# An attention and mixture-of-depths kernel: x stored in halves, weight blocks and mixing at new places, five broadcast loads of 1/rms begun on GpSimd's queue

## The chip, the cores and the metric

The kernel runs on one core of one Trainium2 chip. The core has five engines that each work through their own list of instructions in order: TensorE (PE, matrix products and transposes; PEld in the profile is its weight load), VectorE (DVE), ScalarE (ACT), GpSimd (POOL) and SyncE (SP, here only an issuer of DMA transfers). Engines wait for each other by semaphores. Sixteen DMA engines carry the transfers. The metric is the device time of one execution in microseconds (us); lower is better.

## The reference

The inputs are q, k, v of shape (B 8, H 12, S 448, D 64), the gains g_q and g_k, a gate vector and two matrices of a small network. What is computed:

```
q, k   = rmsnorm(q) * g_q, rmsnorm(k) * g_k        # over D
p      = exp(q k^T / sqrt(D));  x = (p v) / sum(p)  # full attention, no mask
x      -> (B, S, 768)                               # heads side by side
score  = x . w_gate                                 # one number per token
chosen = the 128 tokens of each batch with the highest score
y      = relu(x[chosen] w1) w2                      # 768 -> 1024 -> 768
out    = x, and at the chosen tokens x + sigmoid(score) * y
```

All of it is float32.

## The kernel before

**Groups.** The 96 heads are worked in 24 groups n of four heads; three groups make a batch. A group has seven chunks of 64 keys per head, called units here: `scores` (L404, TensorE) gives the product of keys and queries of one chunk, ScalarE takes its exponential (L413), `values` (L428, TensorE) multiplies by v and accumulates. The main loop runs over q = 0 to 23, one group per round, with `values` trailing `scores` by two or three chunks. PSUM gives `scores` four banks.

**Denominators.** VectorE adds up the probabilities of the chunks (`add_probs`, L444). The last ARRAY[n] chunks of group n are left out of that, and TensorE sums them in `sum_keys` (L471) beside VectorE's sum. `invert_sums` (L496) then forms the reciprocal, and `to_tokens` (L526 transposes on TensorE, L528 products on VectorE) lays the result out by tokens in `xs[b]`, two pieces c = 0 and 1 for each group.

**1/rms.** The norm of the queries of group n is not applied before the scores are due, but as late as possible, in a chain over four engines and a detour by memory: `squares` (L298, ScalarE, sq0 for queries and sq1 for keys), `sum_squares` (L330 on VectorE, then the power of -0.5 at L331 on GpSimd), `rows_out` (L342, SyncE: 1/rms of the queries written to DRAM as rows), `rows_in` (L354: two loads hh = 0 and 1 of 224 KB each that spread the rows over 64 partitions, the tile `bc`), and `scale_q` (L363, VectorE: qT times bc). Only then can `scores` of group n start. Groups 0 and 1 are scaled in another way, without the detour. The norm of the keys goes into the exponential as its scale, so the power of sq1 must have ended before that.

**Queue order.** SyncE issues nearly all transfers, one after the other; an issue that must wait holds all that are behind it. The loads of qT and kT wait until the buffer's last reader, the scores of three groups earlier, has ended; v waits likewise for values of three groups earlier, tok (the rows for the squares, two loads per group) for squares of two groups earlier. `rows_in` waits until the rows have landed in DRAM.

**The planner.** Everything beside the loop's fixed order is put in `todo` under a slot: a number whose whole part is the round and whose fraction is the place in it. For q < 8 (FIRST) a round runs its entries at two points, A (0.5) and its end; later rounds at MID 0.4, P0 0.6, P1 0.75 and P2 0.9. Entries that fall between two run points are issued together, in the order of their slots. `prepare(n)` gives the steps of 1/rms default slots, and the table PREPARED overrides them; LOADS overrides the slots of loads, GATES and RANKS those of the gate sums and of the ranking, BLOCKS those of the 14 weight parts (256 to 512 KB each), MIXED those of `mix`.

**The small network.** After a batch's last tokens, `gate` (L554) and `spread` (L567) form the scores of all tokens, `score_rows` (L584) makes them rows, `count` (L600) ranks each token by how many are higher, `select` (L627, GpSimd) writes the chosen tokens to DRAM by four indirect transfers, and `load_selected` (L650) reads them back. `mixture` handles two batches at a time and does each layer with seven block products in place of eight (L753, L823), using sums and differences of weight blocks that `mix` (L292, VectorE) makes once and `store_mixed` and `load_mixed` take to DRAM and back. It is cut into pieces; rounds q >= 8 run one at each of P0, P1 and P2 unless SKIP names the place. The store of a finished x (L542, 1344 KB) is issued in `store_x` as soon as a batch's tokens are complete.

The lines that carry the slots of 1/rms are these:

```
times = {
    "sq0": n - 3 + (END if n - 3 < FIRST else P0),
    "out": n - 2 + (A if n - 2 < FIRST else P0),
    "in": n - 2 + (A if n - 2 < FIRST else P2),
    "scale": n - 1 + (A if n - 1 < FIRST else P0),
}
```

Of the kernel before, what the change touches and what calls it, by code (L numbers as in the profile page):

```python
# [17 lines left out]
def _bcast_row(ap_1d: bass.AP, parts: int) -> bass.AP:  # L18
# [1 line left out]

ARRAY = (0, 0, 1, 2, 3, 2, 2, 2, 1, 0, 0, 2, 1, 0, 0, 0, 0, 0, 0, 0, 0, 0, 0, 0)
GATE_PE = {1}
OTHER_BANK = (8, 12, 14, 15, 17, 20, 21)
SKIP = ((8, 0), (8, 1), (8, 2), (11, 2), (13, 2), (14, 1), (16, 2), (18, 2), (19, 2), (20, 1),
 (21, 1), (22, 1), (23, 1), (23, 2))
MIXED = ((1, 1, 0, 8.9), (1, 1, 1, 8.9), (1, 2, 0, 9.9), (1, 2, 1, 10.3), (1, 3, 0, 10.3),
 (1, 3, 1, 10.3), (1, 0, 0, 10.9), (1, 0, 1, 11.6), (2, 1, 0, 11.9), (2, 1, 1, 11.9),
 (2, 2, 0, 12.6), (2, 2, 1, 12.6), (2, 3, 0, 12.75), (2, 3, 1, 14.3), (2, 0, 0, 14.3),  # L30
 (2, 0, 1, 14.6))
BLOCKS = (2.3, 2.73, 3.16, 3.59, 4.02, 4.45, 4.88, 5.31, 4.74, 6.17, 6.6, 8.03, 7.46, 8.14)
LOADS = {('kT', 21): 19.3, ('tok', 15): 10.7, ('v', 18): 16.91}
PREPARED = {3: {'out': 1.3},
 4: {'in': 2.9, 'out': 2.3},
 5: {'in': 3.9, 'out': 3.3, 'sq1': 3.5, 'sum0': 2.92, 'sum1': 3.89},
 6: {'in': 4.9, 'out': 4.3, 'scale': 5.5},
 7: {'in': 5.9, 'out': 5.3},
 8: {'in': 6.9, 'sum1': 6.89},
 9: {'in': 7.9, 'out': 7.3},  # L40
 10: {'in': 8.9, 'out': 8.3},
 11: {'sum1': 9.75},
 13: {'scale': 12.59},
 14: {'scale': 13.4, 'sum0': 11.62},
 15: {'out': 13.75},
 17: {'in': 15.75},
 18: {'in': 16.92, 'out': 16.61},
 20: {'out': 18.89, 'scale': 19.42},
 22: {'out': 20.59},
 23: {'sq0': 20.76}}  # L50
GATES = {7: (8.9, 9.4),
 8: (9.9, 10.4),
 10: (11.75, 12.6),
 11: (12.9, 13.3),
 13: (15.3, 15.4),
 17: (18.75, 18.9),
 19: (20.9, 21.3),
 20: (21.9, 22.4),
 22: (24.4, 24.4)}
RANKS = {3: (13.6, 13.6, 13.6, 14.4), 5: (19.6, 20.4, 20.4, 20.9), 6: (22.9, 23.4, 23.4, 23.6)}  # L60


MAX_SCORE = 60.0
# [54 lines left out]
def fast(  # L118
# [21 lines left out]
    nc = tc.nc  # L140
# [3 lines left out]
    NJ = S // CP  # L144
# [4 lines left out]
    DM = H * D  # L149
# [7 lines left out]
    scale = 1.0 / math.sqrt(D)  # L157
# [190 lines left out]
    def rows_in(n):  # L348

        rows = bcs[n]  # L350
        bc = norm_pool.tile([128, 2, S], F32, name="bc")
        for hh in range(2):
            src = rows[hh].rearrange("(c s) -> c s", c=2)
            nc.sync.dma_start(  # L354
                out=bc[D * hh : D * (hh + 1)],
                in_=dataclasses.replace(src, ap=[[0, D]] + [list(x) for x in src.ap]),
            )
        bcs[n] = bc
# [35 lines left out]
    probs, sums, avs, xTs, rdens, xs = {}, {}, {}, {}, {}, {}  # L394
# [62 lines left out]
    def by_array(n):  # L457

        return ARRAY[n]

# [58 lines left out]
    def to_tokens(n, c, pool):  # L519
        b = n // NG  # L520
        if b not in xs:
            xs[b] = x_pool.tile([CP, NJ, DX], F32, name="x")
        t = xTs.pop((n, c))
        ps = bank(pool, [128, NJ, 128], "x_ps")
        for j in range(NJ):
            nc.tensor.transpose(out=ps[:CP, j, :], in_=t[:, j, :], identity=ident)  # L526
        col = (n % NG * 2 + c) * 128
        nc.vector.tensor_tensor(  # L528
            out=xs[b][:, :, col : col + 128].rearrange("p j (h d) -> p j h d", d=D),
            in0=ps[:CP].rearrange("p j (h d) -> p j h d", d=D),  # L530
            in1=rdens[n][:, :, :, c, None].to_broadcast([CP, NJ, 2, D]),
            op=OP.mult,
        )
        if c == 1:
            after_tokens(n)
# [2 lines left out]

    gates, parts, rowss, highers, ranks, slots_dram = {}, {}, {}, {}, {}, {}

    def store_x(b):
        nc.sync.dma_start(  # L542
            out=out[b].rearrange("(p j) c -> p j c", j=NJ), in_=xs[b][:, :, 0:DM]
        )

    def gate(n, js):
# [325 lines left out]
    def at(slot, fn, *args):  # L872
        todo.setdefault(slot, []).append(lambda: fn(*args))
# [3 lines left out]
    def soon():  # L877

        return slot[0] if now[0] < n_groups else -9
# [5 lines left out]
    def prepare(n):  # L885
        sq = {}
        times = {
            "sq0": n - 3 + (END if n - 3 < FIRST else P0),
            "sum0": n - 3 + END + 0.03 if n - 3 < FIRST else n - 2 + MID,
            "sq1": n - 2 + A if n - 2 < FIRST else n - 2 + P0 if n - 3 < FIRST else n - 3 + P1,  # L890
            "sum1": n - 2 + END + 0.02 if n - 2 < FIRST else n - 2 + MID,
# [16 lines left out]
        at(times["scale"], scale_q, n)

    for n in range(1, n_groups):  # L910
        if n > 2:
            for i in range(2):
                at(LOADS.get(("tok", n), n - 5 + P2 if n > 5 else (n - 3) * 0.6), load, "tok", n, i)
        if n > 1:
            at(LOADS.get(("qT", n), max(n - 3 + 0.1, 0.3)), load, "qT", n)
            at(LOADS.get(("kT", n), max(n - 2 + A, 0.3)), load, "kT", n)
            at(LOADS.get(("v", n), max(n - 2 + A, 0.3)), load, "v", n)
            prepare(n)
    for k, (l, b) in enumerate([(1, b) for b in kept + ((0, 1),)] + [(2, b) for b in kept]):
        for part in range(2):  # L920
            at(BLOCKS[2 * k + part], load_block, l, b, part)
    for l, i, part, t in MIXED:
        at(t, mix, l, i, part)
# [7 lines left out]
    def after_tokens(n):  # L931
        b, g = divmod(n, NG)
        s = soon()
        if g == NG - 1:
            at(s, store_x, b)
        if b in GATE_PE or g == 0:
            return
        q = now[0]
        if s < 0:
            t = [s, s]  # L940
        elif q < FIRST:
            t = [q + A, q + A] if g == NG - 1 else [q + END, q + END]
        else:
            t = [q + P2, q + 1 + MID]
        t = GATES.get(n, t)
        at(t[0], gate, n, (0, 1))
        at(t[1], gate, n, (2, 3))
        if g == NG - 1:
            at(t[1], spread, b)

    def ranks_of(b):
# [9 lines left out]
        else:  # L961
            times = [q + P2, q + 1 + MID, q + 1 + MID, q + 1 + P2]
            if b not in GATE_PE:
                times = [q + P0, q + P1, q + P1, q + 1 + 0.3]
        times = RANKS.get(b, times)
        at(times[0], count, b, (0, 1))
# [22 lines left out]
    def add_late():  # L989
# [7 lines left out]
        out=gg, in0=loads.gcol[:, 0:1], scalar=scale, in1=loads.gcol[:, 1:2], op0=OP.mult, op1=OP.mult  # L997
# [94 lines left out]
    n = n_groups - 1  # L1092
# [567 lines left out]
```

## Time and profile before

| | |
|---|---|
| median of 6 runs | 505.15 us (504.28 to 506.44) |
| the profiled execution's own time | 506.53 us, span 504.8 us |
| mean granted TensorE clock | 0.989 |
| busy, share of the span | PE 95%, PEld 59%, DVE 74%, ACT 57%, POOL 38% |
| DMA | 118.44 MB, 235 GB/s on average |
| bc: issue to landing | 3.3 / 4.5 / 12.4 us (min, median, max) |
| kT: issue to landing | 4.4 / 6.1 / 8.6 us |
| v: issue to landing | 5.1 / 7.0 / 9.1 us |

The rounds start (first `scores` of the group) at 10.4, 24.3, 36.9, 51.7, 65.7, 82.2, 98.3, 113.7, 127.5 and 143.4 us for q = 0 to 9, then about every 18 to 21 us, the last at 407.2. The profile is read with TensorE first: where it is never idle, only less work on it or a better order of the end can help; where it is idle, the bracket in its timeline names what it waited for, and the waits of the other engines lead back from there. A wait can be put down to the wrong engine when several semaphores end close together, so times of the instructions themselves decide.

### The profile page before, as it was taken

What the parts mean: (1) busy time and instruction counts of PE and PEld (TensorE: products, weight loads), DVE (VectorE), ACT (ScalarE), POOL (GpSimd) and SP (SyncE); (2) the same over time, 40 slices, a digit from 0 to 9 for tenths busy, and PEclk for the clock granted to TensorE, in tenths of its full rate; (3) what the DMA queues carried; (4) which work ended last, traced back from release to release, by engine and by line L of the source; (5) the groups of instructions that cost most, each with busy time, mean ns of one, the idle gap of its engine ahead of it and who ended that gap; (6) DMA issues with size and microseconds to landing.
All of it is one profiled execution on the core that took longest, in us unless ns stands there. A gap on an engine that the chain in (4) does not pass through costs nothing.

```text
span 504.8 us, 11762 instructions
## 1 busy us (share of the span) xinstructions
PE 479.3 (95%) x4716; PEld 295.4 (59%) x4716; DVE 371.8 (74%) x646; ACT 285.3 (57%) x523; POOL 191.7 (38%) x104
## 2 busy tenths in 40 slices
PE   7999998889979999999999999999999999999992
PEld 6553443445438785554556776655655577759951
DVE  5676887658987997888979886789988786743141
ACT  4877777577857647628557666656655663102100
POOL 0785440845753256404554237224445011021003
PEclk9999999999989999999999999999999999999996
DMA  8868989897998694878787698659385504864721
GB/s 292 314 193 284 268 256 311 271 271 244 309 312 255 227 320 160 275 261 280 243 269 262 217 355 260 207 194 309 131 273 203 173 7 137 271 225 162 229 87 67
DMA packets 44865, 118.44 MB, mean 235 GB/s; under 512 B 10147, under 2 KB 10404, under 8 KB 44802
## 3 DMA queue, kind: packets, MB, share of 16 engines
q1 hardware_dynamic: 41170, 110.66, 66.8%
q0 software_dynamic: 3344, 6.71, 3.7%
q8 instruction: 39, 0.64, 0.5%
q10 hardware_dynamic: 288, 0.23, 0.2%
q14 instruction: 24, 0.20, 0.1%
HBM read 93.81 MB, written 31.64 MB: 249 GB/s over the span
## 4 chain that ended last, share of the span: by engine, by line
PE 70%; DMA 4%; DVE 2%; issue 1%; POOL 1%; ACT 0%; SPq 0%; POOLq 0%; DVEq 0%
PE sc L404 17%; PE av L428 17%; PE moe_ps L753 9%; PE moe_ps L823 8%; PE side_ps L823 6%; PE side_ps L753 6%; PE x_ps L526 3%; PE den_ps L471 2%; DMA bc<-rows 2%; PE xeT_ps L729 1%; DMA rows<-rinv 1%; DMA out_dram<-xe,row 1%; PE row_ps L584 1%; POOL out_dram L683 1%; DVE prod L554 0%
## 5 line engine op out<-in xcount | busy, mean ns | idle before, releaser
L413 ACT ACTIVATE p<-sc,rinv 128x448 f32<-128x448 f32 x336 | 187.7, 641 | 88.1 <-PE sc L404 62.9
L331 POOL TENSOR_TENSOR rinv<-ss,neg_half 128x14 f32<-128x14 f32 x46 | 132.2, 2885 | 161.5 <-DVE ss L330 147.2
L404 PE MATMUL sc<-qT,kT 64*64 64x448 f32 x1344 | 155.4, 544 | 9.4 <-ACT sq L298 2.3
L428 PE MATMUL av<-p,v 64*64 64x448 f32 x1344 | 151.5, 539 | 0.0
L444 DVE TENSOR_TENSOR sum<-sum,p 128x896 f32<-128x896 f32 x104 | 113.7, 1094 | 5.3 <-ACT p L413 0.9
L404 PEld LDWEIGHTS sc<-qT,kT 64*64 64x64 f32 x1344 | 58.7, 133 | 72.9 <-issue 40.7
L428 PEld LDWEIGHTS av<-p,v 64*64 64x64 f32 x1344 | 64.3, 134 | 63.2 <-issue 54.6
L627 POOL DMA_INDIRECT selected<-x,rank x32 | 39.9, 1248 | 86.2 <-DVE x L619 78.7
L330 DVE TENSOR_REDUCE ss<-sq 128x14 f32<-128x910 f32 x46 | 48.8, 1093 | 3.6 <-ACT sq L298 3.6
L298 ACT ACTIVATE sq<-tok 128x896 f32<-128x896 f32 (+1 forms) x49 | 44.8, 936 | 8.8 <-DVE ss L330 4.8
L528 DVE TENSOR_TENSOR x<-x_ps,rden 112x512 f32<-112x512 f32 x48 | 32.6, 689 | 15.0 <-PE x_ps L526 12.9
L363 DVE SCALAR_TENSOR_TENSOR qT<-qT,gg,bc 128x896 f32<-128x896 f32 x22 | 25.5, 1161 | 18.2 <-DMA bc<-rows 18.2
L554 DVE SCALAR_TENSOR_TENSOR prod<-x,wg 112x448 f32<-112x448 f32 (+1 forms) x56 | 31.2, 557 | 1.4
L526 PE MATMUL x_ps<-ident,xT 128*112 128x128 f32 x192 | 28.5, 275 | 0.4 <-DVE rden L496 0.4
L444 DVE TENSOR_TENSOR sum<-p 128x896 f32<-128x896 f32 x24 | 26.1, 1087 | 3.5 <-ACT p L413 3.4
L683 POOL DMA_INDIRECT out_dram<-xe,row x7 | 8.4, 1200 | 52.0 <-DVE xe L695 45.8
L451 ACT COPY xT<-av 128x448 f32<-128x448 f32 x48 | 23.3, 538 | 3.7 <-PE av L428 3.2
L526 PEld LDWEIGHTS x_ps<-ident,xT 128*112 128x112 f32 x192 | 21.5, 133 | 4.8 <-issue 2.9
L753 PE MATMUL moe_ps<-xeT,ring 128*128 128x128 f32 x192 | 23.2, 277 | 0.2 <-DVE hT L770 0.2
L600 DVE SCALAR_TENSOR_TENSOR cmp<-score_rows,gate,earlier 112x448 f32<-112x448 f32 x32 | 21.8, 683 | 1.7 <-ACT score_rows L590 1.0
L753 PE MATMUL side_ps<-xeT,w 128*128 128x128 f32 x192 | 22.8, 275 | 0.0
L753 PEld LDWEIGHTS moe_ps<-xeT,ring 128*128 128x128 f32 x192 | 22.1, 192 | 1.0 <-issue 0.5
(106 smaller groups left out, 445.7 us busy)
## 6 DMA issues: line engine op xcount, KB each, us to landing
tok<-in_tok_dram SPq DMA_DIRECT2D x47, 448.0 KB, 6.1
ring<-mixed SPq DMA_DIRECT2D x48, 384.0 KB, 4.0
qT<-in_qT_dram SPq DMA_DIRECT2D x24, 448.0 KB, 4.0
kT<-in_kT_dram SPq DMA_DIRECT2D x24, 448.0 KB, 6.1
v<-in_vp_dram SPq DMA_DIRECT2D x24, 448.0 KB, 7.0
out_dram<-x SPq DMA_DIRECT2D x8, 1344.0 KB, 9.5
bc<-rows SPq DMA_DIRECT2D x44, 224.0 KB, 4.5
mixed<-ring SPq DMA_DIRECT2D x16, 384.0 KB, 5.8
```

The lines of the kernel that those rows point to most:

```text
L298: nc.scalar.activation(out=sq[:, h, :, 0:D], in_=t[:, h], func=AF.Square, scale=scale)
L330: nc.vector.tensor_reduce(out=ss, in_=sq, axis=AX.X, op=OP.add)
L331: nc.gpsimd.tensor_tensor(out=rinv.rearrange(flat), in0=ss.rearrange(flat), in1=neg_half.to_broadcast([128, 2 * NI]), op=OP.pow,)
L404: nc.tensor.matmul(out=scs[hh][D * c : D * (c + 1), 0:S], lhsT=get("kT", n)[r, c, D * i : D * (i + 1)], rhs=get("qT", n)[r, c, :], start=True,
L413: nc.scalar.activation(out=p[:, hh], in_=scs[hh][:, 0:S], func=AF.Exp, scale=rinvs[n, 1][:, hh, i : i + 1],)
L428: nc.tensor.matmul(out=avs[n][c][D * hh : D * (hh + 1), 0:S], lhsT=get("v", n)[r, hh, i, :], rhs=probs[u][r, hh], start=(i == 0), stop=(i ...
L444: nc.vector.tensor_tensor(out=sums[n], in0=probs.pop(u - 1) if begins else sums[n], in1=probs.pop(u), op=OP.add)
L526: nc.tensor.transpose(out=ps[:CP, j, :], in_=t[:, j, :], identity=ident)
L528: nc.vector.tensor_tensor(out=xs[b][:, :, col : col + 128].rearrange("p j (h d) -> p j h d", d=D), in0=ps[:CP].rearrange("p j (h d) -> p j ...
L627: w = nc.gpsimd.indirect_dma_start(out=t[:, :], out_offset=bass.IndirectOffsetOnAxis(ap=rank[:, j : j + 1], axis=0), in_=x[:, j, :], in_of ...
L753: nc.tensor.matmul(out=ps[:, 128 * f : 128 * f + n], lhsT=w[:, d, 128 * f : 128 * (f + 1)], rhs=h[:, d, :n], start=first and f == d == 0, ...
L823: nc.tensor.matmul(out=ps[:n, c0:c1], lhsT=h[:, f, :n], rhs=w[:, f, c0:c1], start=first and f == 0, stop=(f == HF - 1), skip_group_check=True,
```

## The change

Six tables and three small functions change. In words:

- Five of the 44 halves of `rows_in`, named in OTHER_QUEUE as (group, half), are begun on GpSimd's queue and no longer on SyncE's. GpSimd then waits for the rows to land before it goes on with what is behind.
- `store_x` issues a batch's store in two halves, and STORES gives four batches slots of their own for them; the other batches issue both halves where the whole one stood.
- BLOCKS and MIXED: 14 weight parts and 16 mixing steps get other slots, most of the parts later.
- LOADS: some 35 loads get slots of their own, above all qT 4, 6, 7, 9 to 11 and kT 10 to 14 and 16 to 18 later; PREPARED: the steps of 1/rms of most groups move, many `in` and `sq0` earlier.
- ARRAY: group 1 gives TensorE one chunk more, 5 two fewer, 6 one more, 11 one fewer, 12 one more; 16 in all in both. OTHER_BANK, GATES, RANKS and SKIP: other places for a PSUM bank, for gate sums, for ranking steps and for two of the pieces.

```diff
-ARRAY = (0, 0, 1, 2, 3, 2, 2, 2, 1, 0, 0, 2, 1, 0, 0, 0, 0, 0, 0, 0, 0, 0, 0, 0)
+ARRAY = (0, 1, 1, 2, 3, 0, 3, 2, 1, 0, 0, 1, 2, 0, 0, 0, 0, 0, 0, 0, 0, 0, 0, 0)
 GATE_PE = {1}
-OTHER_BANK = (8, 12, 14, 15, 17, 20, 21)
-SKIP = ((8, 0), (8, 1), (8, 2), (11, 2), (13, 2), (14, 1), (16, 2), (18, 2), (19, 2), (20, 1),
- (21, 1), (22, 1), (23, 1), (23, 2))
+OTHER_BANK = (8, 14, 20, 21)
+SKIP = ((8, 0), (8, 1), (8, 2), (11, 1), (13, 2), (14, 1), (16, 2), (18, 2), (20, 1), (22, 0),
+ (22, 1), (22, 2), (23, 1), (23, 2))
+OTHER_QUEUE = ((2, 0), (6, 0), (8, 1), (12, 0), (14, 0))
...
-BLOCKS = (2.3, 2.73, 3.16, 3.59, 4.02, 4.45, 4.88, 5.31, 4.74, 6.17, 6.6, 8.03, 7.46, 8.14)
-LOADS = {('kT', 21): 19.3, ('tok', 15): 10.7, ('v', 18): 16.91}
...
+BLOCKS = (3.55, 5.8, 3.16, 3.66, 4.27, 7.95, 7.13, 8.13, 6.24, 10.92, 6.1, 11.03, 9.71, 9.71)
+LOADS = {('kT', 5): 3.3,
+ ('kT', 10): 8.91,
+ ('kT', 11): 9.91,
+ ('kT', 12): 11.0,
+ ('kT', 13): 11.91,
+ ('kT', 14): 12.91,
+ ('kT', 16): 14.7,
+ ('kT', 17): 16.0,
+ ('kT', 18): 16.3,
+ ('qT', 3): 0.3,
+ ('qT', 4): 1.6,
+ ('qT', 6): 3.3,
+ ('qT', 7): 4.6,
+ ('qT', 8): 4.9,
+ ('qT', 9): 6.6,
+ ('qT', 10): 7.21,
...
+ ('v', 9): 8.0,
...
-PREPARED = {3: {'out': 1.3},
- 4: {'in': 2.9, 'out': 2.3},
- 5: {'in': 3.9, 'out': 3.3, 'sq1': 3.5, 'sum0': 2.92, 'sum1': 3.89},
- 6: {'in': 4.9, 'out': 4.3, 'scale': 5.5},
- 7: {'in': 5.9, 'out': 5.3},
- 8: {'in': 6.9, 'sum1': 6.89},
- 9: {'in': 7.9, 'out': 7.3},
- 10: {'in': 8.9, 'out': 8.3},
...
+PREPARED = {2: {'in': 0.51, 'sum1': 0.91},
+ 3: {'in': 1.5, 'out': 1.3, 'scale': 2.32, 'sq1': 1.3},
+ 4: {'in': 2.9, 'out': 2.3, 'sq0': 1.51},
+ 5: {'in': 3.51, 'out': 3.3, 'scale': 4.32, 'sq1': 3.5, 'sum1': 3.91},
+ 6: {'out': 4.3, 'scale': 5.5, 'sq0': 3.52, 'sq1': 4.29},
+ 7: {'in': 5.51, 'out': 5.3, 'sq0': 4.32},
+ 8: {'in': 6.51, 'out': 6.32, 'scale': 7.5, 'sum1': 6.89},
+ 9: {'sq0': 6.5, 'sq1': 7.5, 'sum1': 7.52},
+ 10: {'scale': 9.89, 'sq0': 7.49, 'sq1': 8.61, 'sum1': 8.61},
...
+ 15: {'out': 13.62, 'scale': 14.76, 'sq0': 12.89},
...
+STORES = {1: (6.9, 7.5), 2: (9.75, 10.75), 4: (15.75, 16.6), 6: (21.75, 22.6)}
...
-            nc.sync.dma_start(
+            queue = nc.gpsimd if (n, hh) in OTHER_QUEUE else nc.sync
+            queue.dma_start(
                 out=bc[D * hh : D * (hh + 1)],
...
-    def store_x(b):
+    def store_x(b, js):
         nc.sync.dma_start(
-            out=out[b].rearrange("(p j) c -> p j c", j=NJ), in_=xs[b][:, :, 0:DM]
+            out=out[b].rearrange("(p j) c -> p j c", j=NJ)[:, js], in_=xs[b][:, js, 0:DM]
         )
...
-            at(s, store_x, b)
+            for js, t in zip((slice(0, 2), slice(2, 4)), STORES.get(b, (s, s))):
+                at(t, store_x, b, js)
```

More of the change, by code (lines that the diff above doesn't have):

```diff
@@ L19, in _bcast_row @@
     return dataclasses.replace(ap_1d, ap=[[0, parts]] + [list(x) for x in ap_1d.ap])
-ARRAY = (0, 0, 1, 2, 3, 2, 2, 2, 1, 0, 0, 2, 1, 0, 0, 0, 0, 0, 0, 0, 0, 0, 0, 0)
+ARRAY = (0, 1, 1, 2, 3, 0, 3, 2, 1, 0, 0, 1, 2, 0, 0, 0, 0, 0, 0, 0, 0, 0, 0, 0)
 GATE_PE = {1}
-OTHER_BANK = (8, 12, 14, 15, 17, 20, 21)
-SKIP = ((8, 0), (8, 1), (8, 2), (11, 2), (13, 2), (14, 1), (16, 2), (18, 2), (19, 2), (20, 1),
- (21, 1), (22, 1), (23, 1), (23, 2))
-MIXED = ((1, 1, 0, 8.9), (1, 1, 1, 8.9), (1, 2, 0, 9.9), (1, 2, 1, 10.3), (1, 3, 0, 10.3),
- (1, 3, 1, 10.3), (1, 0, 0, 10.9), (1, 0, 1, 11.6), (2, 1, 0, 11.9), (2, 1, 1, 11.9),
- (2, 2, 0, 12.6), (2, 2, 1, 12.6), (2, 3, 0, 12.75), (2, 3, 1, 14.3), (2, 0, 0, 14.3),
- (2, 0, 1, 14.6))
@@ L32 @@
-BLOCKS = (2.3, 2.73, 3.16, 3.59, 4.02, 4.45, 4.88, 5.31, 4.74, 6.17, 6.6, 8.03, 7.46, 8.14)
-LOADS = {('kT', 21): 19.3, ('tok', 15): 10.7, ('v', 18): 16.91}
-PREPARED = {3: {'out': 1.3},
- 4: {'in': 2.9, 'out': 2.3},
- 5: {'in': 3.9, 'out': 3.3, 'sq1': 3.5, 'sum0': 2.92, 'sum1': 3.89},
- 6: {'in': 4.9, 'out': 4.3, 'scale': 5.5},
- 7: {'in': 5.9, 'out': 5.3},
- 8: {'in': 6.9, 'sum1': 6.89},
- 9: {'in': 7.9, 'out': 7.3},
- 10: {'in': 8.9, 'out': 8.3},
[L42 to L55, printed above, removed]
+OTHER_BANK = (8, 14, 20, 21)
+SKIP = ((8, 0), (8, 1), (8, 2), (11, 1), (13, 2), (14, 1), (16, 2), (18, 2), (20, 1), (22, 0),
+ (22, 1), (22, 2), (23, 1), (23, 2))
+OTHER_QUEUE = ((2, 0), (6, 0), (8, 1), (12, 0), (14, 0))
+MIXED = ((1, 1, 0, 8.9), (1, 1, 1, 9.9), (1, 2, 0, 9.3), (1, 2, 1, 10.3), (1, 3, 0, 10.3),
+ (1, 3, 1, 10.9), (1, 0, 0, 10.9), (1, 0, 1, 11.6), (2, 1, 0, 11.9), (2, 1, 1, 12.6),
+ (2, 2, 0, 12.6), (2, 2, 1, 12.6), (2, 3, 0, 13.6), (2, 3, 1, 14.6), (2, 0, 0, 14.4),
+ (2, 0, 1, 14.6))
@@ new lines @@
+BLOCKS = (3.55, 5.8, 3.16, 3.66, 4.27, 7.95, 7.13, 8.13, 6.24, 10.92, 6.1, 11.03, 9.71, 9.71)
[15 more added lines that the diff above has]
+ ('qT', 10): 7.21,
+ ('qT', 11): 8.6,
+ ('qT', 18): 15.6,
+ ('qT', 19): 16.6,
+ ('qT', 20): 17.21,
+ ('qT', 21): 18.3,
+ ('tok', 14): 9.5,
+ ('tok', 15): 10.7,
+ ('tok', 19): 15.4,
+ ('tok', 21): 17.4,
+ ('tok', 23): 18.5,
+ ('v', 3): 1.91,
+ ('v', 9): 8.0,
+ ('v', 10): 8.61,
+ ('v', 13): 11.91,
+ ('v', 15): 13.61,
+ ('v', 16): 14.3,
+ ('v', 18): 16.91,
+ ('v', 23): 21.1}
@@ new lines @@
+PREPARED = {2: {'in': 0.51, 'sum1': 0.91},
[7 more added lines that the diff above has]
+ 10: {'scale': 9.89, 'sq0': 7.49, 'sq1': 8.61, 'sum1': 8.61},
+ 11: {'sum0': 8.89},
+ 12: {'in': 10.92, 'scale': 11.74, 'sq0': 9.9},
+ 13: {'in': 11.74, 'scale': 12.6, 'sq0': 10.9, 'sum0': 11.4, 'sum1': 11.61},
+ 14: {'out': 12.62, 'scale': 13.6, 'sum0': 11.74},
+ 15: {'out': 13.62, 'scale': 14.76, 'sq0': 12.89},
+ 16: {'in': 14.74, 'out': 14.59, 'scale': 15.4, 'sq1': 14.4, 'sum1': 14.59},
+ 17: {'in': 15.61, 'sum0': 15.39},
+ 18: {'in': 16.92, 'scale': 17.61, 'sq0': 15.4, 'sq1': 16.4, 'sum0': 15.4},
+ 19: {'sq0': 16.91, 'sum1': 17.4},
+ 20: {'out': 18.76, 'scale': 19.42, 'sq0': 17.42},
+ 21: {'out': 19.75, 'scale': 20.74},
+ 22: {'out': 20.59, 'scale': 21.75},
+ 23: {'in': 21.74, 'out': 21.4, 'sum1': 22.6}}
@@ L56 @@
+STORES = {1: (6.9, 7.5), 2: (9.75, 10.75), 4: (15.75, 16.6), 6: (21.75, 22.6)}
+GATES = {8: (10.4, 10.4),
+ 10: (11.9, 12.75),
+ 11: (12.75, 12.75),
+ 14: (16.3, 16.4),
  17: (18.75, 18.9),
  19: (20.9, 21.3),
- 20: (21.9, 22.4),
- 22: (24.4, 24.4)}
-RANKS = {3: (13.6, 13.6, 13.6, 14.4), 5: (19.6, 20.4, 20.4, 20.9), 6: (22.9, 23.4, 23.4, 23.6)}
+ 20: (21.75, 22.3),
+ 22: (24.3, 24.9)}
+RANKS = {2: (10.9, 10.9, 10.9, 11.3), 5: (19.6, 20.3, 20.3, 20.4), 6: (22.9, 23.4, 23.4, 23.9)}
 MAX_SCORE = 60.0
```

## The prediction

> **What bounds the kernel now.** I read first the busy time by stretch, then the waits, then TensorE's own timeline where it sat idle, then SyncE's queue, and last the chain that ended last. Columns of the first view: stretch, its length, busy us of PE, PEld, DVE, ACT and POOL (instructions in brackets), granted clock, DMA share, GB/s.
>
> ```profile
> 0.00:150.00 150.00, 135.35 (x1618) 69.93 (x1622) 107.88 (x181) 105.95 (x190) 76.06 (x41) 0.99 0.86 277
> 150.00:430.00 280.00, 279.77 (x2738) 176.29 (x2731) 235.46 (x402) 171.05 (x318) 104.64 (x51) 1.00 0.69 229
> 430.00:505.00 75.00, 64.20 (x366) 49.19 (x365) 28.43 (x64) 8.29 (x16) 10.99 (x13) 0.95 0.50 170
> 143.00:150.00 7.00, 6.01 (x38) 2.12 (x42) 6.86 (x13) 3.24 (x6) 4.66 (x1) 0.76 1.02 370
> ```
>
> From 150 to 430 us TensorE is full, and a load that comes sooner is worth nothing there. The tail has 10.8 us of idle TensorE, but the change leaves the last products and writes as they are, and both versions run 34 pieces of the mixture in the loop. What can be won lies before 150 us, where 14.65 us are idle, 10.1 of them in the seven gaps shown below. The last row shows a granted clock of 0.76: in the trace it stands at 0.5 from 145.49 to 148.90 us.
>
> ```profile
> DVE qT L363 <- DMA bc<-rows: 18.2, 8, 4.2
> PEld den_ps L471 <- DVE sum L444: 11.0, 13, 1.7
> ```
>
> All eight of VectorE's waits for `bc` (the broadcast 1/rms) come before 150 us: 3.12 for group 2, then 2.67, 0.31, 2.25, 4.24, 3.86, 0.44 and 1.34 for groups 3 to 9. They reach TensorE directly (`scores` need the scaled qT) or through the sums and gates queued behind the scale:
>
> ```profile
> 44.90 0.59 PE L471 MATMUL den_ps<-sum,pick_pair 128*32 128x112 f32 x16 [0.83 <-DVE sum L444]
> 58.85 0.59 PE L471 MATMUL den_ps<-sum,pick_pair 128*32 128x112 f32 x16 [0.89 <-DVE sum L444]
> 81.67 0.56 PE L584 MATMUL row_ps<-ident,gate 112*112 112x112 f32 x4 [2.12 <-DVE gate L567]
> 98.33 0.98 PE L404 MATMUL sc<-qT,kT 64*64 64x448 f32 x8 [1.86 <-issue]
> 113.66 1.36 PE L404 MATMUL sc<-qT,kT 64*64 64x448 f32 x12 [1.47 <-ACT sq L298]
> 143.35 1.93 PE L404 MATMUL sc<-qT,kT 64*64 64x448 f32 x10 [2.26 <-DVE qT L363]
> 145.92 1.02 PE L404 MATMUL sc<-qT,kT 64*64 64x448 f32 x3 [0.64 <-DVE x L528]
> ```
>
> The gap is in the bracket. The labels at 98.33 and 113.66 mislead: the scale of group 6 ended at 98.23, that of group 7 at 113.56, each 0.1 us before. Why `bc` is late stands in SyncE's queue, which issues strictly in order:
>
> ```profile
> 64.39 0.33 SPq L110 DMA_DIRECT2D qT<-in_qT_dram  x1
> 65.30 0.36 SPq L342 DMA_DIRECT2D rows<-rinv  x1
> 70.74 1.09 SPq L354 DMA_DIRECT2D bc<-rows  x2
> 78.19 0.33 SPq L110 DMA_DIRECT2D qT<-in_qT_dram  x1
> 78.61 0.38 SPq L342 DMA_DIRECT2D rows<-rinv  x1
> 80.52 0.69 SPq L542 DMA_DIRECT2D out_dram<-x  x1
> 83.60 2.50 SPq L354 DMA_DIRECT2D bc<-rows  x2
> ```
>
> At 64.39 qT 6 had waited for the last scores of group 3 (64.32); rows 5, whose 1/rms was ready at 61.99, stood behind it. The same at 78.19: rows 6 were ready at 74.98. Then the 1344 KB store of x and two weight parts go out ahead of bc 6, which lands only at 96.96. So it is also on the chain (start, us, what):
>
> ```profile
> 126.56 3.80 DMA rows<-rinv
> 130.94 11.11 DMA bc<-rows
> 142.14 1.15 DVE qT L363
> ```
>
> **The change, part by part.** The profiled execution took 506.53 us (span 504.8); the median of the six runs is 505.15, 1.38 below. The sum is made against the former and taken off the latter.
>
> *Loads of qT behind rows.* qT 4, 6, 7 and 9 go behind `rows_out` of the group before them. Rows 3 leave about 1.4 us sooner (35.6 for 37.05) and their bc 3 lands near 47 instead of 50.37, before VectorE asks for it at 47.8: the 2.67 us wait goes, and with it the gaps at 51.72 (0.29) and 58.85 (0.89). What was queued behind qT (kT, v, weights) goes no later; qT itself is needed a whole group later, 0.33 us of issue each. Rows 5 leave at about 62.4 for 65.30, bc 5 at about 73 for 78.1; VectorE is ready at 75.9, so the 2.25 us wait goes and the row transposes' 2.12 with it. Next late there is VectorE itself: its gates end 2.2 us sooner.
>
> *bc 6 and bc 7.* Rows 6 leave near 75.7, and no store and fewer weights stand ahead. The rows give a landing of about 2 us plus the queued bytes at 290 GB/s (2.2 MB ahead of bc 7 took 9.4 us); that puts bc 6 near 85 against the 92.8 at which VectorE waits: 1.86 goes. For bc 7 the rows can't leave sooner (its 1/rms ends at 100.67, behind four row writes of the selection on GpSimd), but 512 KB of weights are gone from in front: about 108.5 for 112.4, with VectorE ready at 108.55: 1.47 goes.
>
> *Group 9.* bc 9 goes out directly after its rows; half the store and v 9 stand behind. It lands near 136 for 142.05. The scale then ends where VectorE's copy of x at 140.11 lets it, about 141.95 for 143.29. Of 2.26 + 0.64, between 1.3 (the scale alone) and 2.6 go; I take 2.0. The half clock of 3.41 us costs 1.7 us; gaps of 2.12 and 1.86 before brought none. With a gap near 0.95 left, it goes wholly or stays: 0 to 1.7, I take half, 0.85. The Trainium skill ("TensorE: Matmul & The Clock Gate", What's actually happening) says the clock drops after an idle window of about 3.4 us; here 2.26 and 0.64 us sufficed. By that rule the shorter gap saves all of the 1.7 and the sum ends 0.85 lower; by the row it is open.
>
> *ARRAY.* Group 1 gives one chunk to TensorE: 16 matmuls, about 0.40 us, for an addition of 1.09 us on VectorE. The gap of 0.83 at 44.90 loses 0.43 net. Group 5 gives two back (2.18 us to VectorE, 0.8 off TensorE); its sums then come later: cost 0.25, between 0 and 0.5. The other changes of ARRAY cancel (16 chunks in both).
>
> *Squares and the copy of rows crowd ScalarE at 7.5*: two squares (936 ns each) ahead of exponentials; four `sc` banks cover most. Between 0 and 0.94, I take 0.45. *Scale 15 at the last place of q = 14* ends 0.1 to 0.2 after its scores are due (261.89): 0.15. *Scale 10* ends near 165.25 against 166.01: nothing, its cover 0.76 us. *v 9* now stands behind a tok load that waits for squares: issued near 142.3, it lands at 147.4 by the shortest v (5.1 us), 149.3 by the median (7.0), 151.4 by the longest (9.1). Its values began at 150.96 before and would begin near 148.3 now: 0 to 3.1, I take 0.7, below the median's 1.0 because fewer weights stand in front.
>
> *Five halves of bc on GpSimd's queue.* An issue there is 609 ns in the nearest row (the last `selected` load), 532 ns on SyncE: 3.0 us on an engine 38% busy. It also waits there for its rows to land, ahead of the next powers; on SyncE that wait is 88.8 us in 19, 4.7 each. GpSimd's own idle time before a power is 147.2 us in 22, 6.7 each, so I cost it at nothing; without that cover it would be up to 5 x 4.7 = 23 us on GpSimd. SyncE saves 5 x 0.53 = 2.7 us. The Trainium skill ("DMA: Bandwidth & Descriptors", Issuing engines are not separate DMA queues) speaks against more: whoever starts a transfer, it runs on the same 16 engines. By it this part moves no landing and the sum stands; by the row of bc 6, whose two issues took 2.50 us, half of it would begin 1.25 us sooner and the sum could end that much lower.
>
> *Stores in halves*: the same bytes, eight more issues, 8 x 0.66 (0.69 and 0.63 in two rows) = 5.3 us of SyncE, hidden while it waits on scores (99.1 us in 19). *Weights and mixes later*: 1.6 MB leave the first 150 us (5.5 us of DMA at 290 GB/s, booked above); VectorE's mixes, gates and counts are only moved, as are the banks of OTHER_BANK and the steps in SKIP. *kT 10 to 14 and 16 to 18 half a group later*: kT 17 goes out near 286.5, lands 6.1 us later near 293, and is wanted at 299.14; kT 10 lands near 158 for 166.01. Nothing, with 6 us of cover. For the rest (some forty moved entries in a stretch with TensorE full) 0 to 2, I take 1.0.
>
> **Sum.** 0.43 + 0.29 + 0.89 + 2.12 + 1.86 + 1.47 + 2.0 + 0.85 = 9.91 gained; 0.25 + 0.45 + 0.15 + 0.7 + 1.0 = 2.55 lost: 7.36. Profiled 506.53 - 7.36 = 499.2; median 505.15 - 7.36 = 497.8.
>
> **The rivals.** A, bc 6, 7 and 9 stay late: DMA share is 1.01 from 82 to 98 us and 0.94 from 127 to 143, and qT 8 still holds SyncE until 95.04 (the last scores of group 5). Only the early gaps go: 0.43 + 0.29 + 0.89 + 2.12 = 3.7, so 501.4 (500.3 to 503.6). Against it: bc 6's issue itself is 2.9 us sooner. B, everything goes, the clock too: 0.83 + 0.29 + 0.89 + 2.12 + 1.86 + 1.47 + 2.26 + 0.64 + 1.7 = 12.1, so 493.1. Against it stands VectorE's x at 140.11. C, the moves hide nothing, new waits eat what is won: 505. D, slower: the eight moved kT loads land after their scores are due. Landing times run 4.4 to 8.6 us, the wait on squares adds to that. It decides from 8.9 us in all (7.36 + 1.5), 1.1 each; at 1.5 each 505.15 - 7.36 + 12 = 509.8. Against it: 6 us of cover.
>
> **How the numbers follow.** Main 0.57 (495.2 to 500.3, its losses between 0 and twice what I took), A 0.20, B 0.09, C 0.05, D 0.09. A measurement of this kernel tells 0.3%, 1.5 us, from no change. Faster: main, A and B, 0.86; same C; slower D. The range 493.5 to 503.6 leaves out C, D and half of B, 0.18.
>
> **What would show it.** Right: VectorE's waits for `bc` before 150 us fall from 18.2 to under 6; no gap over 0.5 us ahead of the row transposes near 80 and of scores 6 and 7; a chain without an 11 us `bc`; PE busy of the first 143 us up. A shows in bc 7 and 9 landing over 9 us after issue. D shows as `PE sc` waiting on DMA kT between 150 and 320 us. The clock row near 145 settles the 0.85. Wrong would be a PE idle of more than 2 us between 150 and 430, or GpSimd's powers ending later and rows waiting for them.

## The result and the profile after

The changed kernel takes 500.84 us (median of 20 runs, 497.35 to 503.99); the kernel before, run beside it, 504.63 (46 runs). The ratio is 0.9915, with a 95% interval from 0.9898 to 0.9933: 4.3 us faster, where 7.36 were forecast (the two medians by themselves are 3.8 apart).

The profiled execution took 500.34 us (span 498.4, clock 0.993), 6.19 below the one before; the spans differ by 6.4. That has three parts. The first scores start 0.79 us sooner: ScalarE's first wait for a tok load was 0.93 us for 1.70, and over all fourteen profiles here the first scores start anywhere from 9.47 to 10.53 us, so the start is chance. The time from the first scores of group 0 to those of group 23 is 4.4 us shorter. The end, from the last group's first scores on, is 1.20 us shorter (96.42 for 97.62), and this is not chance: see the run a_all_oneq. The profiled execution before was 1.9 us above the median of its kernel, so the pair of profiles shows a larger gain than the medians; which part of it that is, isn't shown, but a half clock worth 1.7 us, which comes and goes between executions, is in that profile.

Busy time by stretch, in the columns of before:

```profile
0.00:150.00 150.00, 142.33 (x1724) 75.02 (x1724) 113.06 (x190) 112.12 (x201) 80.04 (x46) 1.00 0.82 274
150.00:430.00 280.00, 276.95 (x2677) 175.29 (x2667) 233.45 (x408) 165.09 (x307) 100.86 (x50) 1.00 0.71 236
143.00:150.00 7.00, 7.00 (x99) 4.90 (x95) 6.76 (x11) 5.35 (x10) 3.96 (x2) 1.00 0.88 306
```

TensorE is busy for 142.33 of the first 150 us, 7 more than before, but the full stretch is no longer full: 3 us are idle in it. The half clock near 145 us (a granted TensorE clock of 0.5) is gone. The wait for the broadcasts, and TensorE where it still sat idle or stretched:

```profile
DVE qT L403 <- DMA bc<-rows: 10.9, 5, 5.6
```
```profile
93.58 2.39 PE L444 MATMUL sc<-qT,kT 64*64 64x448 f32 x16
...
107.62 1.74 PE L444 MATMUL sc<-qT,kT 64*64 64x448 f32 x16 [3.20 <-issue]
136.78 1.93 PE L444 MATMUL sc<-qT,kT 64*64 64x448 f32 x10 [0.83 <-DVE qT L403]
139.34 0.60 PE L444 MATMUL sc<-qT,kT 64*64 64x448 f32 x3 [0.64 <-DVE x L568]
216.70 0.65 PE L566 MATMUL x_ps<-ident,xT 128*112 128x128 f32 x4 [1.47 <-DVE rden L536]
```

The gaps at 44.90, 51.72, 58.85, 81.67 and 98.33 have no successor. The one before scores 7.0 (at 107.62; scores n.0 are the first scores of group n) has grown from 1.47 to 3.20 us, half of all that VectorE still waits for `bc` (5.58 of 10.9) belongs to it, and one of 1.47 us has come up in round 12, which had none. The rounds, from first scores to first scores (worked out from the two timelines, us):

| round q | 2 | 3 | 4 | 5 | 6 | 7 | 8 | 9 | 10 | 11 | 12 | 13 | 14 |
|---|---|---|---|---|---|---|---|---|---|---|---|---|---|
| before | 14.80 | 13.97 | 16.47 | 16.17 | 15.33 | 13.79 | 15.90 | 22.66 | 20.92 | 18.24 | 20.90 | 18.27 | 17.55 |
| changed | 13.02 | 13.02 | 14.17 | 14.17 | 17.10 | 14.69 | 14.47 | 21.20 | 20.92 | 18.77 | 22.19 | 18.65 | 18.09 |

Seven us are won up to scores 6.0; rounds 6 and 7 give 2.7 back; 8 and 9 win 2.9; 11 to 14 give back 2.7; later rounds sum to the same.

VectorE is ready for the scale of group 7 when its addition ends, and then waits for `bc`. First the kernel before, then the changed one:

```profile
107.47 1.08 DVE L444 TENSOR_TENSOR sum<-p 128x896 f32<-128x896 f32 x1
112.41 1.15 DVE L363 SCALAR_TENSOR_TENSOR qT<-qT,gg,bc 128x896 f32<-128x896 f32 x1 [3.86 <-DMA bc<-rows]
```
```profile
99.71 1.08 DVE L484 TENSOR_TENSOR sum<-p 128x896 f32<-128x896 f32 x1
106.37 1.15 DVE L403 SCALAR_TENSOR_TENSOR qT<-qT,gg,bc 128x896 f32<-128x896 f32 x1 [5.58 <-DMA bc<-rows]
```

Where the loss of round 6 comes from is read from GpSimd and ScalarE, then SyncE:

```profile
82.96 1.04 POOL L667 DMA_INDIRECT selected<-x,rank  x1 [5.07 <-DVE x L659]
88.08 1.76 POOL L667 DMA_INDIRECT selected<-x,rank  x1 [0.31 <-issue]
89.85 10.50 POOL L370 TENSOR_TENSOR rinv<-ss,neg_half 128x14 f32<-128x14 f32 x4
```
```profile
92.73 2.21 ACT L453 ACTIVATE p<-sc,rinv 128x448 f32<-128x448 f32 x4 [1.43 <-POOL rinv L370]
```
```profile
95.29 0.33 SPq L381 DMA_DIRECT2D rows<-rinv  x1
97.86 0.38 SPq L690 DMA_DIRECT2D xe<-selected  x1
98.54 1.10 SPq L394 DMA_DIRECT2D bc<-rows  x2
```

The four writes of batch 0's selection hold GpSimd from 82.96 to 89.84. The power of sum1 6 follows, and the exponentials of group 6 wait 1.43 us for it (hence the 2.39 us scores); only then comes the power of sum0 7 (its sum was ready at 84.67), so SyncE stands 4.7 us for it and rows 7 leave at 95.29; bc 7 follows as soon as they have landed. Meanwhile the DMA engines had little to do: their share, the last column but one, was 0.41 and then 0.16 from 86 to 90 us.

```profile
86.00:88.00 2.00, 2.00 (x28) 0.88 (x24) 2.00 (x3) 1.73 (x4) 1.77 (x1) 1.00 0.41 143
88.00:90.00 2.00, 2.00 (x26) 0.63 (x15) 1.90 (x3) 1.18 (x3) 1.91 (x2) 1.00 0.16 49
```

### The profile page after: what moved, and what is told of

Read it like the earlier page. It is cut to its first block, busy times and chain, and to the rows that moved or that the text cites. A ratio compares the mean times of both kernels' runs of the same rounds, so it can differ in the third digit from the quotient of the medians.

```text
span 498.4 us, 11761 instructions
## 1 busy us (share of the span) xinstructions
PE 479.0 (96%) x4716; PEld 295.4 (59%) x4716; DVE 370.5 (74%) x646; ACT 284.9 (57%) x523; POOL 191.9 (39%) x109
## 5 line engine op out<-in xcount | busy, mean ns | idle before, releaser
L370 POOL TENSOR_TENSOR rinv<-ss,neg_half 128x14 f32<-128x14 f32 x46 | 129.0, 2815 | 136.1 <-DVE ss L369 111.4
L403 DVE SCALAR_TENSOR_TENSOR qT<-qT,gg,bc 128x896 f32<-128x896 f32 x22 | 25.2, 1146 | 10.9 <-DMA bc<-rows 10.9
```

Of the source, the lines that this page charges most:

```text
L370: nc.gpsimd.tensor_tensor(out=rinv.rearrange(flat), in0=ss.rearrange(flat), in1=neg_half.to_broadcast([128, 2 * NI]), op=OP.pow,)
```

## The experiments

Each set of four shared its runs of the kernel before, on one chip; ratios are to those. The chips differ between the sets, so rounds and gaps in the profiles decide more than ratios across sets.

### First set: why the gap before scores 7.0 grew

**b_in6**, one gap taken from the kernel before:

```diff
-LOADS = {('kT', 21): 19.3, ...
+LOADS = {('qT', 7): 4.6, ('kT', 21): 19.3, ...
- 6: {'in': 4.9, 'out': 4.3, 'scale': 5.5},
+ 6: {'out': 4.3, 'scale': 5.5},
```

> The kernel before with one change: qT 7 is loaded at 4.6 and the two bc loads of group 6 are issued at 4.5, so that rows 6 no longer stand behind qT 7 and bc 6 no longer behind the store of x and the weight parts. Theory M (a later gap is measured against a deadline that moves with the gaps won ahead of it): bc 6 lands before 90 us, the gap before scores 6.0 falls from 1.86 to under 0.3 us, and the gap before scores 7.0 grows from 1.47 to about 3.3 us, because 1/rms 7 comes out of GpSimd at the same time as before, behind the four writes of the selection; time within 0.15% of before. Rival (gaps add): the gap before scores 7.0 stays near 1.5 us and the time falls by 1.9 us, to 0.9963 of before.

Ratio 1.0044 (1.0019 to 1.0070).

```profile
78.70 0.56 PE L584 MATMUL row_ps<-ident,gate 112*112 112x112 f32 x4 [0.55 <-DVE gate L567]
...
111.84 2.11 PE L404 MATMUL sc<-qT,kT 64*64 64x448 f32 x10 [3.74 <-issue]
```

There is no gap before scores 6.0 any more, and round 5 also starts sooner (the row transposes wait 0.55 us for 2.12, an effect that was not expected). The gap before scores 7.0 is 3.74 us. Scores 6.0 start 4.9 us sooner than before, scores 7.0 only 1.8: the gap took 2.3 of it, and the second scores of group 6 most of the rest (2.39 us for 1.71, as in the changed kernel). At scores 8.0 the kernel stands at 127.32 us, the one before at 127.45: all that two gaps had given is gone, the last 1.7 of it by a half clock. Theory M's gap is confirmed, its time is not: it came out 2.2 us slower. In the profile two stretches of half clock, after the gap of 3.74 and after one of 2.59 before scores 9.0, took more than before (granted clock 0.66 from 111 to 115 us and 0.57 from 142 to 150).

**b_in6_pow**, with the powers ahead of the selection:

```diff
+ 6: {'out': 4.3, 'scale': 5.5, 'sum1': 4.86},
+ 7: {'in': 5.9, 'out': 5.3, 'sq0': 4.32, 'sum0': 4.85},
```

> The kernel before with the same change, and also sq0 of group 7 at 4.32 and the powers of sum1 6 (4.86) and sum0 7 (4.85) ahead of the ranking and selection of batch 0 on VectorE and GpSimd. Theory M: both gaps go, under 0.7 us each, the power of sum0 7 ends before 90 us; time falls by about 3 us, to 0.994 of before. Rival (bc 7 is late by its own transfer and the bytes ahead of it): the gap before scores 7.0 stays over 2 us, and the time does not differ from the run without the earlier powers.

Ratio 0.9946 (0.9914 to 0.9978), 5 us below b_in6; in the profiles round 6 is 3.0 us shorter than there, and round 7, where b_in6 had a half clock, 1.6. The power of sum0 7 ends at 87.74; the gap before scores 7.0 is 1.55, between what the two theories said. Rows 7 left at 91.71 behind qT 8, and bc 7 was issued at 100.93, directly behind the load of the selected tokens at 100.50.

**a_pow**, the same two powers in the changed kernel:

```diff
- 6: {'out': 4.3, 'scale': 5.5, 'sq0': 3.52, 'sq1': 4.29},
- 7: {'in': 5.51, 'out': 5.3, 'sq0': 4.32},
+ 6: {'out': 4.3, 'scale': 5.5, 'sq0': 3.52, 'sq1': 4.29, 'sum1': 4.86},
+ 7: {'in': 5.51, 'out': 5.3, 'sq0': 4.32, 'sum0': 4.85},
```

> The changed kernel with the powers of sum1 6 (4.86) and sum0 7 (4.85) ahead of the ranking and selection of batch 0. Theory M: the power of sum0 7 ends before 84 us, the gap of 3.20 us before scores 7.0 falls under 1 us and the second scores of group 6 no longer stretch to 2.39 us (its exponentials waited for the power of sum1 6); time 3 to 4 us below the changed kernel, some 0.985 of before. Rival (transfer and bytes): rows 7 leave sooner but bc 7 still lands within 1.5 us of where it did, the gap stays over 2 us, time at most 1 us below the changed kernel.

Ratio 0.9878 (0.9842 to 0.9913), some 2 us below the changed kernel where 3 to 4 were expected.

```profile
91.57 0.44 SPq L381 DMA_DIRECT2D rows<-rinv  x1
99.19 0.33 SPq L690 DMA_DIRECT2D xe<-selected  x1
99.62 1.09 SPq L394 DMA_DIRECT2D bc<-rows  x2
```
```profile
106.54 1.74 PE L444 MATMUL sc<-qT,kT 64*64 64x448 f32 x16 [2.00 <-issue]
```

Round 6 is 15.09 us for 17.10, and the second scores of group 6 take 1.68 us for 2.39. The two powers ended at 86.55 (84 was expected). The powers were a cause, but not the whole: the gap fell to 2.00 and not below 1, because SyncE waits 6.0 us for the selection, now later, at the load of the selected tokens (99.19), and bc 7 stands behind that load.

**a_mix**: `(2, 1, 1, 12.6)` back to `(2, 1, 1, 11.9)` in MIXED.

> The changed kernel with the second mixing step of block (2, 1) back at 11.9, where it is in the kernel before. Theory: the gap of 1.47 us before the token transposes at 216.7 us comes from three mixing steps and a scale in a row on VectorE ahead of the reciprocal; with one of the three gone (0.95 us) it falls to about 0.5 us and the time by about 0.9 us, 0.990 of before. Rival: VectorE is so full there that the step taken away makes something else late, and the time does not change.

Ratio 0.9939 (0.9911 to 0.9967). The gap was 1.25 us, and the time not below the changed kernel's 0.9915; but the profile also has a gap of 0.99 us in round 2 and a half clock in round 7, which the edit doesn't touch, so the lines decide and not the time. First the mixing line of the changed kernel, then the two of this run:

```profile
201.77 0.96 DVE L331 TENSOR_TENSOR ring<-ring,w 128x768 f32<-128x768 f32 x1 [2.55 <-DMA ring<-in_w_dram]
```
```profile
203.12 0.96 DVE L331 TENSOR_TENSOR ring<-ring,w 128x768 f32<-128x768 f32 x1 [1.66 <-DMA ring<-in_w_dram]
204.67 0.96 DVE L331 TENSOR_TENSOR ring<-ring,w 128x768 f32<-128x768 f32 x1 [0.59 <-DMA ring<-in_w_dram]
```

The step moved back waits for the same weight block (2.25 us in all), so VectorE is late all the same. The theory (too many steps in a row) fell: the step's place isn't it; that it is the block's arrival is the next guess, not shown here.

### Second set: what was late next, and the named parts undone

**a_pow_sel**, a_pow with `RANKS = {0: (4.9, 4.9, 4.9, 5.6), ...`:

> The changed kernel with the two powers moved up as in the run a_pow, and also the load of the selected tokens of batch 0 at 5.6 in place of 5.5, so behind the bc loads of group 7. Theory S (SyncE stood at that load until the selection had landed, and bc 7 behind it): the bc loads of group 7 are issued before 96 us for 99.6, the gap before scores 7.0 falls from 2.00 to under 0.7 us; time 1 to 1.5 us below a_pow, some 0.985 of before. Rival (the wait for scores 5.6 in the load of qT 8, ahead of rows 7, is what holds it): bc 7 is issued within 1 us of where it was and the time is that of a_pow, 0.988.

Ratio 0.9820 (0.9778 to 0.9862). bc 7 was issued at 96.67 for 99.62 (not quite before 96) and TensorE has no gap before scores 7.0. Theory S holds: no other edit separates it from a_pow. A half clock came in round 9 (22.85 us for 21.20). The gap near 213 us was 0.41 here, though nothing was done for it.

**a_all**, a_pow_sel with two more edits:

```diff
- ('qT', 8): 4.9,
+ ('qT', 8): 5.35,
-RANKS = {0: (4.9, 4.9, 4.9, 5.6), 2: (10.9, 10.9, 10.9, 11.3), ...
+RANKS = {0: (4.9, 4.9, 4.9, 5.6), 2: (10.9, 10.9, 10.9, 11.95), ...
```

> As a_pow_sel, and also qT 8 loaded at 5.35 (behind rows 7) and the load of the selected tokens of batch 2 at 11.95 in place of 11.3 (behind rows 13 and the weight block of layer 2 that the mixing at 201.8 us waited 2.55 us for). Theory S: no gap before scores 7.0 over 0.3 us; VectorE's wait for the ring block goes, and with it the gap of 1.47 us before the token transposes near 216 us (under 0.5); time 3 us below a_pow, some 0.982 of before. Rival (VectorE is simply full in that round): the gap near 216 stays over 1 us and the time is that of a_pow_sel.

Ratio 0.9810 (0.9769 to 0.9852), median 496.04 us. Round 6 is now 13.02 us:

```profile
103.08 0.60 PE L566 MATMUL x_ps<-ident,xT 128*112 128x128 f32 x4
103.61 1.74 PE L444 MATMUL sc<-qT,kT 64*64 64x448 f32 x16
```

Rows 7 left at 86.42 and bc 7 was issued at 90.89. VectorE no longer waits for the ring block and round 12 is 20.51 us for 22.19. Round 12 takes 20.51 in all four kernels that have this edit, and from 20.63 (a_pow) to 22.19 in the seven changed ones without it. So the edit may help, but since 20.63 came without it, it is not shown to be the cause.

**a_oneq**, the changed kernel with `OTHER_QUEUE = ()`:

> The changed kernel with all bc loads on SyncE's queue. Theory: the queue alone moves no landing that TensorE waits for; every gap of the changed kernel stays within 0.5 us and the time is that of the changed kernel, 0.990 to 0.994 of before. Rival G (the five loads on GpSimd save landings): bc 6 or bc 8 lands later by 1 us or more, a new gap appears before scores 6.0 or 8.0, time 1 to 2 us above the changed kernel. Rival H (GpSimd's wait for the rows delays its powers): the powers behind end sooner and the time is 1 us or more below the changed kernel.

**a_whole**, the changed kernel with `at(s, store_x, b, slice(0, 4))` for the loop over halves:

> The changed kernel with each batch's x stored whole where the kernel before stores it (no halves, no slots of their own). Theory: the store is behind the bc loads of group 9 in both, so bc 9 lands within 1 us of where it did and the time is that of the changed kernel, 0.990 to 0.994 of before. Rival: the halves are what lets bc 9 and bc 7 through; with whole stores VectorE waits for bc 9 again by over 1 us and the time rises by 1.5 us or more, half clock included.

Ratios 0.9970 (0.9939 to 1.0000) and 0.9952 (0.9919 to 0.9984): slower than expected, but by something that neither theory named. In both, TensorE crept through the denominators of group 4; these lines are from a_oneq:

```profile
84.91 0.43 PE L511 MATMUL den_ps<-p,pick_pair 128*32 128x112 f32 x4 [0.33 <-issue]
85.67 0.40 PE L511 MATMUL den_ps<-p,pick_pair 128*32 128x112 f32 x5 [0.33 <-issue]
87.17 0.40 PE L520 MATMUL den_ps<-xT,hT 128*32 128x112 f32 x4 [0.34 <-issue]
```

Round 5 took 21.55 and 20.33 us for 14.17, the half clock that followed included, and round 6 then only 13.02, with no gap before scores 7.0. All other rounds up to 9 were those of the changed kernel within 0.5 us. There is no gap before scores 6.0 or 8.0 in either, and before scores 9.0 the same 0.83 as in the changed kernel.

### Third set: the slow stretch, and the parts undone without it

**a_same**, the changed kernel itself.

> The changed kernel itself once more, beside the runs below. In the runs a_oneq and a_whole TensorE crept through the small products of the denominators of group 4 between 84 and 89 us (four or five at a time, 0.3 us apart, put down to issue), which the profile of the changed kernel doesn't show. Theory R (this comes and goes from run to run or chip to chip, and hits the changed kernel too): times spread over 5 us or more and the median is 0.990 to 0.997 of before. Rival K (it belongs to the two kernels with one part undone): the profile shows no such stretch and the ratio stays at 0.990 to 0.993.

Ratio 0.9913 (0.9881 to 0.9946), as in the result, a spread of 4.6 us, and no slow stretch in the profile. That speaks for K, but the ratio lies in R's range too, and one profile can't rule out what comes and goes. Also, this set ran on another chip than a_oneq and a_whole, so whether the stretch belongs to those kernels or to that chip stays open; two kernels of the same set on the same chip, a_pow_sel and a_all, did not have it, and there the selection is written after those products. The gap before scores 7.0 was 3.59 us here, and this time it cost a half clock too (granted clock in the third column from the right):

```profile
108.00:110.00 2.00, 2.00 (x16) 0.80 (x19) 1.90 (x3) 1.02 (x2) 0.00 (x0) 0.70 1.03 392
110.00:112.00 2.00, 2.00 (x16) 0.98 (x12) 1.90 (x7) 1.30 (x3) 0.00 (x0) 0.50 0.99 390
```

Round 7 was 16.38 us for 14.69.

**a_all_oneq**, a_all with `OTHER_QUEUE = ()`; **a_all_whole**, a_all with whole stores; **a_all_blocks**, a_all with BLOCKS of the kernel before.

> The run a_all with all bc loads on SyncE's queue. Its selection is written after the products of the denominators, so the slow stretch should not come. Theory (the queue is worth nothing here): gaps as in a_all within 0.4 us, time within 0.3% of a_all's 0.981 of before. Rival G (GpSimd's queue is worth 1 to 2 us): bc 6 or 8 late, a gap of over 0.8 us before scores 6.0 or 8.0, 0.983 to 0.986.

Ratio 0.9842 (0.9802 to 0.9882), in rival G's range. But G's gap did not come: every round up to 13 is as long as in a_all within 0.3 us, so begun on SyncE's queue the five loads land in time as well. What the queue is worth lies at the very end, where no `bc` is loaded. GpSimd's last writes, first in a_all and then in a_all_oneq:

```profile
486.93 0.96 POOL L723 DMA_INDIRECT out_dram<-p,row  x1 [2.82 <-DVE p L735]
```
```profile
487.00 0.96 POOL L723 DMA_INDIRECT out_dram<-p,row  x1 [3.43 <-DMA out_dram<-xe,row]
```

That is 89.73 and 90.56 us after the last group's first scores, and the end follows 96.4 and 97.5 us after them. It is so in every profile: with the five loads on GpSimd's queue (nine profiles) the end takes 96.21 to 96.66 us, without them (the kernel before, b_in6, b_in6_pow, a_oneq, a_all_oneq) 97.45 to 97.63. Without them GpSimd waits 3.42 to 3.46 us, put down to the landing of the write ahead, with them 2.81 to 3.02. So the queue is worth about 1.1 us, in GpSimd's last writes, some 0.6 of it in that wait; why five loads begun long before change it stays open.

> The run a_all with each batch's x stored whole, where the kernel before stores it. Theory (the halves are worth nothing here): gaps as in a_all within 0.4 us, time within 0.3% of a_all's 0.981 of before. Rival (the halves let loads through): a gap of over 0.8 us more before scores 7.0 or 9.0, 0.983 to 0.986.

Ratio 0.9797 (0.9765 to 0.9830), median 494.60 us, the lowest of all, though its interval overlaps that of a_all. Up to 13 the rounds are as long as in a_all within 0.3 us, except round 9: 22.79 for 21.20, with a half clock after the gaps of 0.83 and 0.64. The halves are worth nothing that these runs can tell.

> The run a_all with the 14 weight parts at the slots of the kernel before. Theory W (1.6 MB more before 150 us at some 290 GB/s, 5.5 us of DMA, stand ahead of bc 5 to bc 7): VectorE waits again for bc 5, 6 or 7, gaps of together 2 us or more before scores 6.0 and 7.0 and the row transposes; time 2 to 4 us above a_all, 0.985 to 0.989 of before. Rival (order matters, not bytes): the rows leave as early as in a_all, gaps together under 0.8 us, 0.980 to 0.983.

Ratio 0.9852 (0.9807 to 0.9897). The gap of 2.15 us before scores 7.0 is back (round 6 is 15.24 for 13.02), and none before scores 6.0 or the row transposes. Theory W's gap came, at bc 7 alone, and its ratio touches the low end; of the 2.2 us lost in round 6 the spans keep 0.9 (494.5 for 493.6), as rounds 8, 11 and 14 were together 1.15 us shorter than in a_all. The DMA engines were busier (a share of 1.03 from 88 to 96 us, for 0.84 in a_all), SyncE stood 2.9 us for rows 7 to land, and bc 7 was issued at 96.30 for 90.89. Bytes in front matter, then, but here at this one load only.

## Why the prediction was right and wrong

The direction, the range and the bound (SyncE's order ahead of late broadcasts) were right; the size was 0.58 of what was forecast. The 500.84 us lie above the main account's own bounds (495.2 to 500.3) and within those given to rival A. Of the signs named, PE busy of the first 143 us went up (135.33 for 129.34), but VectorE's waits for `bc` fell to 10.9 and not under 6, and a gap of 3.20 stood before scores 7.0; two signs of being wrong came in part: 3.05 us of idle TensorE between 150 and 430 us, the longest gap 1.47, and rows that waited for GpSimd's power, though that power ended sooner than before (95.26 for 100.67). By its own steps:

- *Loads of qT behind rows, bc 3 and bc 5.* 0.29 + 0.89 + 2.12, and 0.43 for ARRAY, make 3.73; rounds 2, 3 and 4 are 5.03 us shorter (1.78, 0.95, 2.30). Right, a little low: round 2 gained 0.66 beyond its two gaps, as its second scores took 1.68 us for 2.47 (before, ScalarE stood 1.55 us for a tok load ahead of the exponentials). No run undoes these moves alone; that they are the cause is read from the queue's times.
- *bc 6.* 1.86 forecast, round 5 shorter by 2.00. Right; b_in6 shows it in the kernel before, where the same order takes the gap away.
- *bc 7: the step that failed.* The text gave 1.47 us, with bc 7 landing near 108.5 and "VectorE ready at 108.55". bc 7 did come sooner, its scale starts 6.0 us before (106.37 for 112.41), and rows 7, which "can't leave sooner", left at 95.29 for 100.69, since the selection moved forward with the rounds. But 108.55 is VectorE's time in the kernel before; with the gaps ahead gone, VectorE was ready at 100.79, 7.8 us sooner. So the gap grew by 1.73 where 1.47 should have gone, and with the exponentials waiting for the power of sum1 6 round 6 lost 1.77, although two chunks of group 5 fewer saved TensorE 0.8 there: 1.47 not gained and 1.77 lost, 3.24 us off the sum. The text had seen that 1/rms 7 stands behind the selection's writes on GpSimd, and then priced the transfer. b_in6 shows the same in the kernel before: the gap of group 6 taken away, that of group 7 grows from 1.47 to 3.74.
- *Group 9 and the half clock.* 2.0 and 0.85 forecast; round 8, with the gap, is 1.43 shorter and round 9, with the half clock, 1.46. The gap left is 0.83 (0.95 forecast), with the 0.64 after it unchanged. That the two make 2.89 for 2.85 is luck: the gap gave less than forecast, and the half clock, which was in the profiled execution before and not in this one, more than the half that was taken.
- *Losses.* Round 7 is 0.90 longer: beside the two squares the last scores took 1.45 us for 0.93 (0.45 forecast for it), and 0.4 is group 6's extra chunk. The additions of group 5 (0.25) made no gap. Scale 15 and the rest, 1.15, stand against 2.74 in rounds 11 to 14, of which 1.29 came in round 12, where VectorE waited for the weight block (in the other changed kernels without a_all's edits the round took from 20.63 to 21.98). v 9 cost nothing that a gap shows.
- *The five loads on GpSimd's queue, the stores in halves, the end.* Costed at nothing, and nothing is what the halves brought in a_all_whole, and the queue in the rounds of a_all_oneq. But the end, which the prediction took as unchanged, is 1.2 us shorter, and a_oneq and a_all_oneq lose 1.1 of it again: a gain that the sum does not have. The rule weighed from the Trainium skill ("DMA: Bandwidth & Descriptors", Issuing engines are not separate DMA queues), that the issuer gives no bandwidth of its own, agrees with the rounds of a_all_oneq. The other one ("TensorE: Matmul & The Clock Gate", What's actually happening: a window of about 3.4 us without work) doesn't: these runs show half clocks after shorter gaps, down to 0.83 and 0.64 us.
- *Rivals.* A was half right: bc 7 stayed late, bc 6 and bc 9 did not, and the time lies beside its 501.4. Its sign did not come: no `bc` took over 7.5 us from issue to landing. It named qT 8, which does hold SyncE (to 89.59), but the power held rows 7 longer, to 95.29, and once the powers are moved the load of the selected tokens holds bc 7 (a_pow). D didn't come: no kT load was waited for.

Against the main sum, 7.36 less 3.24 for bc 7 is 4.1, where the rounds of the profiled pair gained 4.4; what the other terms missed nearly cancels there, which is luck too. The end's 1.2 us come on top; the two make 5.6 in this pair of profiles, where the medians and the ratio give 3.8 to 4.3.

## What to carry to other kernels

A gap is the distance between two times, and both move: if gaps are closed early in a run, every later deadline comes forward, and a late transfer whose own chain (here a GpSimd engine that serves two chains in order) doesn't come forward by as much turns up with a larger gap. So put the sum on a running clock: for each later gap ask by how much the needed time moves and by how much the supplied time moves, and only then subtract. And when a stall is traced to a queue, follow the chain one engine further: the wait here passed from SyncE's order to GpSimd's and back to SyncE's, and only when both were mended was it gone.

## What the runs showed that was not expected

- The half clock is not a matter of one gap's length. A gap of 3.20 us before scores 7.0 brought none in one execution of the changed kernel; one of 3.59 brought it in another, and one of 2.72 in a_mix. Gaps of 0.83 and 0.64 brought it in a_all_whole and a_pow_sel, and not in a_all. Where it came it lasted 3.41 us, or twice that, and 3.41 us of it cost 1.6 to 1.7 us (round 7: 16.38 for 14.69; round 9: 22.79 for 21.20). It can make some of the changed kernel's spread (497.35 to 503.99); how much isn't shown.
- TensorE can issue small products at four to five in some 0.74 us (a_oneq, 84 to 89 us) where 16 take 0.41 us otherwise. The trace names no releaser, and what slowed the issue stays open; it happened while GpSimd wrote the selection (82.84 to 87.76 us).
- Five loads begun on GpSimd's queue before 220 us shorten the kernel's end by 1.1 us, with the same products and writes there (a_all_oneq).
- A version better than both came of the tests: the changed kernel with two powers, two loads of selected tokens and qT 8 reordered stands at 0.981 (0.977 to 0.985) of before, and with whole stores at 0.980 (0.977 to 0.983).
